# Issuing the early gate/up weight loads from GpSimd's DMA queue in place of SyncE's

## Chip, cores and metric

The kernel runs on one core of one Trainium2 chip. The metric is device time in microseconds (us); lower is better. Every kernel was run several times. A ratio is the mean time of one kernel's fast runs over the mean time of the other's fast runs of the same rounds, so it is not quite the ratio of the medians that are quoted beside it. The record marks each run as fast or as fallen into a slower state of the chip.

## The reference

```python
def reference(A_x, A_wqkv, A_wo, B_x, B_W_gate, B_W_up, B_W_down):
    # x: 1 x 2048 x 1024, bf16;  W_gate, W_up: 1024 x 3584;  W_down: 3584 x 1024
    x = A_x
    h  = x + attn(_layernorm(x), A_wqkv, A_wo)      # linear attention, 32 heads of 32
    h2 = h + ffn(_layernorm(h), B_W_gate, B_W_up, B_W_down)
    return h2
    # attn: num/den of phi(q)·(phi(k)^T v), then @ wo
    # ffn:  (relu(x @ W_gate) * (x @ W_up)) @ W_down
```

(Shortened: `attn` and `ffn` stand for the code of the two blocks.)

## The kernel before

The matrix products are done in blocks by Strassen's scheme. Between about 150 and 291 us of the span one stage mixes two things. Token blocks of 128 go through attention: `nd` and `attn` matmuls, the residual, the second layernorm. Beside them run the last q projections (`L438`) and the first gate/up products (`L705`, "early quads"), which fill TensorE. The weights of these early quads come in eight loads of 512 KB. This is the part that loads them:

```python
def hold(dst, src):
    nc.gpsimd.tensor_copy(out=dst, in_=src)            # 1x1 copy, L142

def load_group(g):
    for nm, v in (("wg", wg_v), ("wu", wu_v)):
        w_sb = wpools[g % 2].tile([P, KC, 2, GP * P], BF16, tag=nm, name=nm)
        for h in range(2):
            def load(after=None, w_sb=w_sb, v=v, h=h):
                if after is not None:
                    hold(w_sb[0:1, 0, h, 0:1], after)  # paces the load
                nc.sync.dma_start(out=w_sb[:, :, h, :],            # L486
                                  in_=v[:, :, h, g * GP * P:(g + 1) * GP * P])
            ...
# in the loop over attention steps:
        attn_step(step)
        if step:
            for _ in range(-(-len(early_loads) // (QSTEPS - step))):
                early_loads.pop(0)(held[step][0:1, 0:1])   # after = an element of this step's o_sb
```

So a load goes out only when a 1x1 copy has read this step's attention output `o_sb`. Eight loads are paced over seven steps; I call them the first to the eighth. The SyncE queue also carries everything that a token needs:

```python
nc.sync.dma_start_transpose(out=st["oT"], in_=st["o"][:])                  # L525, "oT transpose"
nc.sync.dma_start(out=x_sb[:], in_=xf[t * P:(t + 1) * P, :])               # L529
nc.sync.dma_start(out=h_dram[i][s][:, r // P, :], in_=h_sb[:])             # L546
# second layernorm: VectorE writes the mean (L551), then ScalarE:
st["hn"] = bwork.tile([P, D], BF16, tag="hn", bufs=HB, name="hn")          # HB = 2 buffers
nc.scalar.activation(out=st["hn"][:], in_=h_sb[:], func=ACT.Square, ...)   # L553
...
nc.sync.dma_start_transpose(out=hnT[s][i][:, :, r:r + P], in_=st["hn"][:]) # L560, "hn transpose"
```

Two users wait for an hn transpose. ScalarE can write an `hn` buffer again (`L553`) only when the transpose has read it, and there are two buffers. VectorE's sums `hs` (`L117`) and the early quads on TensorE read what it wrote.

## Time and profile before

| | before |
|---|---|
| time, median of 3 runs | 745.43 us (742.85 to 746.01) |
| span of the profiled run | 740.6 us |
| PE busy | 721.8 us, 97% |
| attention stage, 152.64 to 291.11 us | 138.47 us, PE idle 7.08 us in it |
| second hn transpose, issue to landing | 4.9 us |

From the page of before: the busy time of each engine, and the chain of waits by engine. In the first line, PE is TensorE's matmuls and PEld its weight loads.

```profile
...
PE 721.8 (97%) x3967; PEld 382.0 (52%) x4020; DVE 563.2 (76%) x991; ACT 322.0 (43%) x580; POOL 5.7 (1%) x44
...
PE 78%; DVE 8%; ACT 7%; DMA 5%; issue 2%; SPq 0%; DVEq 0%; POOL 0%; ACTq 0%
...
```

TensorE bounds the kernel. The next fence is one row of the table of stretches of before: the attention stage, from the issue of the first oT transpose to the first matmul of the next stage (`accA`). PEclk is the clock that the throttle granted TensorE, as a share of full speed.

```profile
...
core 0: us, PE busy (x) PEld busy (x) DVE busy (x) ACT busy (x) POOL busy (x), PEclk, DMA share, GB/s
152.64:291.11 138.47, 131.39 (x669) 62.04 (x681) 104.27 (x262) 95.16 (x241) 1.89 (x8) 1.00 0.75 175
...
```

138.47 less 131.39 gives 7.08 us of idle TensorE, at full clock. The next fence holds a line of the SyncE queue's own waits between 150 and 210 us: total, times, longest. This wait for GpSimd's pacing copies is what the change aims at.

```profile
...
SPq L486 <- POOL wu L142: 8.0, 3, 5.8
...
```

The last two fences are from the timeline of before: start, duration, engine and line. In brackets is how long the engine had waited, and for what. First, the second hn transpose and what hangs on it:

```profile
...
175.92 1.43 SPq L560 DMA_TRANSPOSE hn<-hn  x1
...
177.44 0.58 SPq L486 DMA_DIRECT2D wg<-in_B_W_gate_dram  x1
...
180.90 1.15 ACT L553 ACTIVATE hn<-x_res,sm 128x1024 bf16<-128x1024 bf16 x1 [0.74 <-DMA hn<-hn]
...
186.28 1.46 PE L438 MATMUL Aq<-xT,tq 128*128 128x512 bf16 x5 [1.10 <-ACT u L154]
...
```

The sixth load stands behind the hn transpose on the queue, issued 1.5 us later. ScalarE waits 0.74 us for the transpose (buffer reuse). ScalarE works in order, so its next copy of a PSUM tile (`u`, `L154`) is late, and TensorE waits 1.10 us for that. Second, the eighth load and the fifth hn transpose:

```profile
...
198.19 0.38 SPq L486 DMA_DIRECT2D wu<-in_B_W_up_dram  x1
...
200.97 1.68 SPq L560 DMA_TRANSPOSE hn<-hn  x1
...
204.93 0.43 DVE L117 TENSOR_TENSOR hs<-hn 128x512 f16<-128x512 bf16 x1 [0.26 <-DMA hn<-hn]
...
```

Here the load was issued 2.8 us ahead, and VectorE waits 0.26 us for the transpose.

### The profile page before, as it was taken

The numbers are of one execution on the slowest core, as the hardware profiler recorded it, in microseconds if no ns is written. First come the engines' busy times: TensorE is split into PE (matmuls) and PEld (weight loads), VectorE is DVE, ScalarE is ACT, GpSimd is POOL, SyncE is SP. The second block draws the span as 40 slices with busy tenths as digits, with TensorE's granted clock in tenths as the row PEclk, the third lists the DMA queues.
The fourth block names the chain that finished last, engine by engine and source line by source line (L and its number), as shares of the span: only waits on it lengthen the run. The fifth ranks groups of instructions, "written<-read, shape, count | busy, mean of one in ns | idle before, by whom it ended". The sixth has DMA issues, their size and how long they took to land.

```text
span 740.6 us, 10570 instructions
## 1 busy us (share of the span) xinstructions
PE 721.8 (97%) x3967; PEld 382.0 (52%) x4020; DVE 563.2 (76%) x991; ACT 322.0 (43%) x580; POOL 5.7 (1%) x44
## 2 busy tenths in 40 slices
PE   7999999999989999999999999999999999999997
PEld 3444555444444444444444444444444458888666
DVE  6997653675887767778778777877787479996797
ACT  4786553778686654444344434443435120000000
POOL 0000000000000000000000000000000000000000
PEclk9999999999999999999999999999999999999999
DMA  9765003079797526164638359475483399988822
GB/s 319 167 140 157 0 1 107 9 155 242 152 223 165 138 73 203 46 181 137 196 127 233 109 181 288 162 221 201 170 271 127 124 396 345 326 286 298 300 79 79
DMA packets 146579, 132.03 MB, mean 178 GB/s; under 512 B 50912, under 2 KB 128096, under 8 KB 146528
## 3 DMA queue, kind: packets, MB, share of 16 engines
q1 hardware_dynamic: 135392, 123.23, 55.3%
q10 hardware_dynamic: 11136, 8.13, 3.4%
q8 instruction: 31, 0.51, 0.3%
q14 instruction: 20, 0.16, 0.1%
HBM read 79.95 MB, written 39.85 MB: 162 GB/s over the span
## 4 chain that ended last, share of the span: by engine, by line
PE 78%; DVE 8%; ACT 7%; DMA 5%; issue 2%; SPq 0%; DVEq 0%; POOL 0%; ACTq 0%
PE accA L785 22%; PE accX L785 8%; PE accY L785 8%; PE accA L1117 8%; PE Aq L298 3%; PE accA L946 3%; PE accX L1117 3%; PE Aq L438 3%; DMA hn<-hn 2%; PE accY L1117 2%; PE attn L541 2%; PE Aq L705 2%; PE Eq L298 2%; PE accY L946 2%; PE accX L946 2%
## 5 line engine op out<-in xcount | busy, mean ns | idle before, releaser
L795 ACT ACTIVATE gu<-gu 128x512 bf16<-128x512 bf16 x72 | 45.4, 631 | 131.5 <-DVE gu L794 131.5
L790 ACT COPY snap<-accA 128x1024 f32<-128x1024 f32 x72 | 72.5, 1008 | 36.3 <-PE accA L785 36.2
L785 PEld LDWEIGHTS <-tg 128*128 128x128 f16 x384 | 37.6, 98 | 45.3
L785 PEld LDWEIGHTS <-tu 128*128 128x128 f16 x384 | 37.6, 98 | 45.3
L541 PE MATMUL attn<-wo_mem,oT 128*128 128x512 bf16 x249 | 57.9, 379 | 1.2 <-DVE o_sb L518 0.4
L794 DVE TENSOR_TENSOR gu<-accY,snap 128x1024 bf16<-128x1024 f32 x36 | 43.9, 1219 | 10.0 <-ACT snap L790 10.0
L785 PE MATMUL accA<-hn,tu 128*128 128x512 f16 (+1 forms) x192 | 49.3, 379 | 0.0
L785 PE MATMUL accA<-hn,tg 128*128 128x512 f16 (+1 forms) x192 | 49.3, 379 | 0.0
L794 DVE TENSOR_TENSOR gu<-accX,snap 128x1024 bf16<-128x1024 f32 x36 | 43.9, 1219 | 6.2 <-PE accX L785 3.7
L154 ACT COPY u<-Aq 128x512 f32<-128x512 f32 x56 | 32.4, 582 | 37.3 <-PE Aq L298 19.3
L1117 PEld LDWEIGHTS <-x 128*128 128x128 f16 (+1 forms) x448 | 43.8, 98 | 5.5
L785 PEld LDWEIGHTS <-wg 128*128 128x128 bf16 x288 | 28.2, 98 | 34.0
L785 PEld LDWEIGHTS <-wu 128*128 128x128 bf16 x288 | 28.2, 98 | 34.0
L541 PEld LDWEIGHTS <-oT 128*128 128x128 bf16 x256 | 24.6, 98 | 30.8 <-issue 2.9
L798 DVE TENSOR_TENSOR hq<-gu 128x512 bf16<-128x512 bf16 x48 | 20.3, 423 | 14.3 <-ACT gu L795 14.2
L298 PEld LDWEIGHTS <-xT 128*128 128x128 bf16 (+1 forms) x192 | 18.6, 98 | 23.7 <-issue 2.3
L1117 PEld LDWEIGHTS <-xs 128*128 128x128 f16 x280 | 27.4, 98 | 3.2
L543 DVE SCALAR_TENSOR_TENSOR x_res<-attn,x_res 128x512 bf16<-128x512 f32 x32 | 21.8, 687 | 7.2 <-PE attn L541 7.1
L946 PEld LDWEIGHTS <-x 128*128 128x128 bf16 (+1 forms) x168 | 16.4, 98 | 19.6
L518 DVE TENSOR_TENSOR o_sb<-nd,rd 128x384 bf16<-128x384 f32 (+1 forms) x48 | 22.8, 507 | 4.5 <-ACT rd L517 4.4
L1123 DVE TENSOR_TENSOR snap<-accA,u 128x1024 f32<-128x1024 f32 x16 | 19.5, 1220 | 8.3 <-PE accA L1117 8.0
L785 PE MATMUL accA<-hn,wu 128*128 128x512 bf16 x96 | 24.6, 379 | 0.0
(232 smaller groups left out, 1400.8 us busy)
## 6 DMA issues: line engine op xcount, KB each, us to landing
x<-x_dram SPq DMA_DIRECT2D x17, 896.0 KB, 8.2
x_dram<-hq SPq DMA_DIRECT2D x28, 512.0 KB, 3.1
wg<-in_B_W_gate_dram SPq DMA_DIRECT2D x14, 512.0 KB, 5.2
wu<-in_B_W_up_dram SPq DMA_DIRECT2D x14, 512.0 KB, 7.3
wraw<-in_B_W_down_dram SPq DMA_DIRECT2D x14, 512.0 KB, 4.8
x_dram<-hq SPq DMA_DIRECT2D x28, 256.0 KB, 2.6
t_dram<-wt SPq DMA_DIRECT2D x28, 256.0 KB, 2.2
xd<-x_dram SPq DMA_DIRECT2D x6, 896.0 KB, 7.1
```

The source lines that it names most:

```text
L154: nc.scalar.copy(out=snaps[nm, v], in_=A[v][:])
L298: nc.tensor.matmul(ps[:], lhsT=left[m - 1][:, kc, r + v * P:r + (v + 1) * P], rhs=right[m - 1][:, kc, :], start=(start and kc == 0), stop= ...
L438: nc.tensor.matmul(ps[:], lhsT=rq[m - 1][:, kc, (c + v) * P:(c + v + 1) * P], rhs=left[m - 1][:, kc, :], start=(start and kc == 0), stop=( ...
L518: nc.vector.tensor_tensor(out=ov[:, c0:c0 + n], in0=ndv[:, :, 0:P].rearrange("p k (h e) -> p k h e", h=HPC), in1=rd[:, 0:n, :].unsqueeze(3 ...
L541: nc.tensor.matmul(ps[:], lhsT=st["oT"][:, c, :], rhs=wo_sb[:, c, j * NW:(j + 1) * NW], start=(c == 0), stop=(c == KC - 1))
L543: nc.vector.scalar_tensor_tensor(out=h_sb[:, j * NW:(j + 1) * NW], in0=ps[:], scalar=1.0, in1=h_sb[:, j * NW:(j + 1) * NW], op0=ALU.mult, ...
L785: nc.tensor.matmul(ps[:, v, :], lhsT=w[v][n - 1][:, kc, :], rhs=left[n - 1][:, kc, :], start=(t is not None and kc == 0), stop=(kc == KH - ...
L790: nc.scalar.copy(out=st[nm][:], in_=halves(st["A"]))
L794: add(out=g[:], in0=halves(st[nm]), in1=st[base][:], op=ALU.add)
L795: nc.scalar.activation(out=g[:, 0, :], in_=g[:, 0, :], func=ACT.Relu)
L946: nc.tensor.matmul(ps[:, t * NW:(t + 1) * NW], lhsT=x_tile(n, s, kh)[:, f, (t0 + t) * P:(t0 + t + 1) * P], rhs=w_tile(n, kh)[:, f, :], sta ...
L1117: nc.tensor.matmul(pv[:, tt, :], lhsT=left(m)[:, f, tt * P:(tt + 1) * P], rhs=right(m)[:, f, :], start=(t is not None and f == 0 and tt % ...
```

## The change

The intent is to take the eight paced loads off the SyncE queue, where waiting for the pacing copy blocks the transposes behind. GpSimd makes the copy anyway, so it can issue the load right behind it.

```diff
                 def load(after=None, w_sb=w_sb, v=v, h=h):
                     if after is not None:
                         hold(w_sb[0:1, 0, h, 0:1], after)
-                    nc.sync.dma_start(out=w_sb[:, :, h, :], in_=v[:, :, h, g * GP * P:(g + 1) * GP * P])
+                    (nc.sync if after is None else nc.gpsimd).dma_start(out=w_sb[:, :, h, :], in_=v[:, :, h, g * GP * P:(g + 1) * GP * P])
```

The scheduler also reorders a little. On VectorE the first of the four `hs` sums (`L117`) of the fifth token moves ahead of the mean (`L551`) of the sixth, and the same happens once more two tokens later; some weight sums move later, and two neighbouring groups of matmuls swap on TensorE. ScalarE's order stays.

## The prediction

> **What bounds the kernel now.** TensorE. The page of before gives PE 721.8 us busy of a 740.6 us span (97%), clock 1.0, and the chain of waits is 78% PE. The change touches only the attention/early-quad stage, about 150 to 292 us. By the table of stretches PE is idle about 7 us of 142 there: 1.2 us in 170-190, 2.7 in 210-220, 1.2 in 260-280, the rest in crumbs. A perfect repair is worth 7 us (0.9%); 2% (15 us) is out of reach.
>
> **What it removes.** Eight loads of 512 KB leave the SyncE queue. In the queue's own waits they stood 8.4 us for the GpSimd copies (longest 5.8, ending at 198.2 us); their issue took 0.37 to 0.58 us each, about 3.7 us. Transposes queued near them took 1.75 to 3.24 us to issue where others take 1.23; about 7 us more. SyncE is relieved of 15-19 us between 153 and 200 us.
>
> **What of that is critical.** Little. Most waits of that queue are for data (37.3 us for o_sb). After the longest block (192-198 us) the next attention transpose needed an o_sb that VectorE finished at 199.6, and issued at 199.68. One hn transpose, ready at 198.3, issued at 200.97: 2.6 us earlier is possible. But VectorE is packed from 193 to 205 (9.4-9.5 busy of 10), so the next token's statistics come no sooner. The wait at 220.3 us (PE 2.0 us for the hs sums) ends on the transpose issued at 215.62, when no load is left in either kernel. The 1.1 us wait at 186.3 goes back to an hn transpose (175.92, 4.9 us to land) that shares the DMA engines with a load; the Trainium skill's "DMA: Bandwidth & Descriptors", section "Issuing engines are not separate DMA queues", says that the engines stay shared whoever issues. Expected gain: 0 to 2 us.
>
> **What it adds.** GpSimd, idle here but for eight copies of 0.18-0.3 us, now generates descriptors: 1024 rows of 512 B per load. Before has no such issue; call its duration T. GpSimd is in order, so each copy waits for the issues ahead, and the built code makes VectorE's write of an o_sb buffer wait for the copy that read it two steps before. From before's times (first copies 153.4, o_sb writes 169.5, 174.6, 186.9, 197.2) I estimate that T up to 7 us costs nothing (153.4+3T < 174.6); the weights are first needed at 193.7, so four loads fit up to T of 10. My guess for T is 1.5 to 5 us. The Trainium skill's "SBUF — State Buffer", the box on the "DVE blocks DMA" trap, says that VectorE's two-port modes starve such issues; before cannot show it. Scheduling also moves one hs sum ahead of a token's statistics on VectorE (0.5 us either way).
>
> **Predicted.** 744.5 us (745.43 before), 739.5 to 751.5 eight times in ten. Faster by over 2%: 0.01; within 2%: 0.94; slower: 0.05.
>
> **What would show it.** SyncE's waits for these copies gone, transposes near 1.23 us; eight DMA issues on GpSimd of 1.5-5 us; PE busy unchanged; idle in 150-292 us still 5-9 us; the wait of about 2 us for hs before the first Eq sums still there; stages after 292 us alike but shifted.
>
> **What would make it wrong.** T above 7 us: o_sb writes wait for GpSimd, PE for nd and attn, and tens of us may go. Descriptor writing that slows VectorE's two-input operations (their means would rise). Or an hn loop really SyncE-bound, when up to 5 us come back.

## The result, and the profile after

| | before | after |
|---|---|---|
| time, median of 4 runs of the same rounds | 744.65 us (742.85 to 746.01) | 755.0 us (754.65 to 755.37) |
| ratio, 95% interval | | 1.0141 [1.0116, 1.0165] |
| span of the profiled run | 740.6 us | 753.1 us |
| PE busy | 721.8 us | 729.8 us |
| attention stage | 138.47 us | 150.74 us |
| second hn transpose, issue to landing | 4.9 us | 7.2 us |

The change costs 10.4 us by the medians, outside the predicted range. From the page of after, the busy line and the new queue of GpSimd (packets, MB, share of the 16 engines):

```profile
...
PE 729.8 (97%) x3967; PEld 384.2 (51%) x4020; DVE 563.0 (75%) x991; ACT 322.0 (43%) x580; POOL 12.9 (2%) x52
...
q0 software_dynamic: 1152, 4.19, 2.3%
...
```

The two traces lack the same number of matmul records (3967 of 4020 are there), so their PE times can be compared: 8.0 us more for the same work. VectorE's busy time did not grow. In the view of the load's line after (durations min/median/max in ns), GpSimd's issuing is short and even:

```profile
...
L486 POOL DMA_DIRECT2D wg<-in_B_W_gate_dram x4: 882/883/1018, 153.9 to 176.0; - x4
L486 POOL DMA_DIRECT2D wu<-in_B_W_up_dram x4: 882/883/884, 158.1 to 203.8; - x4
...
```

SyncE's waits for the copies are gone. So the change did what it was meant to do, and the loss is elsewhere. These are rows of the table of stretches of after: the attention stage, then four of the stretches of 2 us around its first stall (columns as in before):

```profile
...
152.91:303.65 150.74, 138.36 (x669) 63.97 (x681) 104.14 (x262) 95.19 (x241) 9.08 (x16) 0.94 0.68 161
...
186.00:188.00 2.00, 0.26 (x2) 0.00 (x0) 1.04 (x2) 2.00 (x3) 0.00 (x0) 0.91 0.29 106
188.00:190.00 2.00, 0.92 (x2) 0.40 (x3) 1.24 (x4) 1.76 (x9) 0.00 (x0) 0.50 0.46 125
190.00:192.00 2.00, 2.00 (x6) 0.73 (x5) 1.39 (x3) 1.24 (x2) 1.06 (x2) 0.50 0.72 145
...
194.00:196.00 2.00, 2.00 (x10) 0.88 (x9) 1.13 (x4) 0.00 (x0) 0.00 (x0) 0.88 1.22 162
...
```

The stage took 12.27 us more, which is the whole difference of the spans within 0.3 us. PE idle in it is 150.74 - 138.36 = 12.38 us, so 5.3 us more. The same 669 matmuls took 138.36 - 131.39 = 7.0 us longer: the clock was halved three times. Before had 1.00 in all these rows. The timeline of after, the first stall:

```profile
...
175.99 0.88 POOL L486 DMA_DIRECT2D wg<-in_B_W_gate_dram  x1 [0.30 <-POOL wg L142]
176.21 1.46 SPq L560 DMA_TRANSPOSE hn<-hn  x1
...
183.48 1.15 ACT L553 ACTIVATE hn<-x_res,sm 128x1024 bf16<-128x1024 bf16 x1 [3.06 <-DMA hn<-hn]
...
188.86 0.58 PE L438 MATMUL Aq<-xT,tq 128*128 128x512 bf16 x1 [2.60 <-ACT u L154]
...
```

The sixth load is now issued at the same moment as the hn transpose, not behind it. The transpose lands after 7.2 us instead of 4.9. ScalarE waits 3.06 us, TensorE 2.60 us, and the clock halves. The second stall:

```profile
...
203.79 0.88 POOL L486 DMA_DIRECT2D wu<-in_B_W_up_dram  x1 [0.30 <-POOL wu L142]
...
204.10 1.27 SPq L560 DMA_TRANSPOSE hn<-hn  x1
...
210.28 0.42 DVE L117 TENSOR_TENSOR hs<-hn 128x512 f16<-128x512 bf16 x1 [2.75 <-DMA hn<-hn]
...
210.86 1.15 ACT L553 ACTIVATE hn<-x_res,sm 128x1024 bf16<-128x1024 bf16 x1 [2.65 <-DVE sm L551]
211.35 0.34 PE L511 MATMUL nd<-kvz,pq_mem 128*128 128x132 bf16 x3 [2.79 <-DVE o_sb L518]
...
```

The eighth load again meets an hn transpose, whose landing took 6.2 us (3.9 before). VectorE waits 2.75 us for it. In the new order the mean `sm` stands behind the first of those sums, so ScalarE waits too, and TensorE 2.79 us.

The third stall, at 226 to 230 us, is of another kind, for before has it too. Here are TensorE's two waits at this place, before and then after:

```profile
...
218.06 0.28 PE L511 MATMUL nd<-kvz,pq_mem 128*128 128x132 bf16 x2 [0.76 <-DVE o_sb L518]
220.34 0.59 PE L705 MATMUL Eq<-hs,tg 128*128 128x512 f16 x2 [2.00 <-DVE hs L117]
...
```

```profile
...
227.91 1.17 PE L511 MATMUL nd<-kvz,pq_mem 128*128 128x132 bf16 x8 [1.89 <-DVE o_sb L518]
230.44 1.01 PE L705 MATMUL Eq<-hs,tg 128*128 128x512 f16 x2 [1.36 <-DVE hs L117]
...
```

Together they grew only from 2.76 to 3.25 us. What is new is the halved clock. VectorE waits 2.92 us for the hn transpose here (0.84 before), but that transpose is hardly later: it landed after 5.4 us, 4.7 before, and 5.5 in two kernels below that lose nothing (six_pool, hb3_before). So a late landing does not explain this third part.

### The profile page after: what moved, and what is told of

Read it like the earlier page. It is cut to its first block, busy times and chain, and to the rows that moved or that the text cites. A ratio compares the mean times of both kernels' runs of the same rounds, so it can differ in the third digit from the quotient of the medians.

```text
span 753.1 us, 10572 instructions
## 1 busy us (share of the span) xinstructions
PE 729.8 (97%) x3967; PEld 384.2 (51%) x4020; DVE 563.0 (75%) x991; ACT 322.0 (43%) x580; POOL 12.9 (2%) x52
## 4 chain that ended last, share of the span: by engine, by line
PE 79%; DVE 8%; ACT 6%; DMA 5%; issue 2%; SPq 0%; DVEq 0%; ACTq 0%
PE accA L785 22%; PE accY L785 8%; PE accX L785 8%; PE accA L1117 8%; PE Aq L298 4%; PE attn L541 3%; PE accA L946 3%; PE accX L1117 3%; PE Aq L438 3%; PE accY L1117 2%; DMA hn<-hn 2%; PE Eq L298 2%; PE Aq L705 2%; PE accY L946 2%; PE accX L946 2%
## 5 line engine op out<-in xcount | busy, mean ns | idle before, releaser
L541 PE MATMUL attn<-wo_mem,oT 128*128 128x512 bf16 x249 | 61.6, 396 | 1.0 <-DVE o_sb L518 0.4
```

What stands on the lines that cost most here:

```text
L541: nc.tensor.matmul(ps[:], lhsT=st["oT"][:, c, :], rhs=wo_sb[:, c, j * NW:(j + 1) * NW], start=(c == 0), stop=(c == KC - 1))
```

## The experiments

Theory A: a load that GpSimd issues no longer stands behind the hn transpose on the SyncE queue. It runs beside it, the transpose lands late, ScalarE or VectorE waits, TensorE gets a gap, and its clock halves. Rival B: the new order on VectorE costs the time. Rival C: descriptor writing slows VectorE; this fell at once (563.2 us busy before, 563.0 after). Rival D: loads from GpSimd cost, whenever they run.

The experiments start from before or from after and differ from them by what their diffs show. "Exact order" means that TensorE, VectorE and ScalarE were compared and have the same instruction order as the kernel named. Where loads are picked out, this numbering was added to the loader:

```diff
-                def load(after=None, w_sb=w_sb, v=v, h=h):
+                def load(after=None, w_sb=w_sb, v=v, h=h, k=4 * g + 2 * (nm == "wu") + h):
```

| run | time, median | before, same rounds | ratio [95%] | second hn transpose lands after |
|---|---|---|---|---|
| sp_behind | 744.1 | 744.26 | 0.9991 [0.9958, 1.0024] | 4.7 us |
| pool_old_order | 749.71 | 744.26 | 1.0061 [1.0025, 1.0097] | 7.3 us |
| one_pool5 | 752.0 | 744.26 | 1.0098 [1.0051, 1.0145] | 11.1 us |
| six_pool | 744.09 | 742.62 | 1.0011 [0.9993, 1.0029] | 4.8 us |
| two_pool | 757.68 | 742.62 | 1.0184 [1.0156, 1.0211] | 9.3 us |
| pool_landed | 747.72 | 742.62 | 1.0060 [1.0034, 1.0086] | 4.8 us |
| early_pool | 748.53 | 742.62 | 1.0068 [1.0052, 1.0085] | 4.2 us |
| sp_ahead | 747.63 | 743.94 | 1.0042 [1.0026, 1.0058] | 6.1 us |
| one_act5 | 745.82 | 743.94 | 1.0026 [1.001, 1.0041] | 6.7 us |
| sp_later | 743.75 | 744.35 | 0.9993 [0.9971, 1.0014] | 4.4 us |
| hb3_before | 743.2 | 744.4 | 0.9984 [0.9969, 0.9999] | 4.6 us |
| hb3_one5 | 747.92 | 744.4 | 1.0055 [1.0023, 1.0086] | 12.2 us |
| hb3_old | 748.39 | 744.4 | 1.0051 [1.0035, 1.0066] | 7.1 us |
| hb3 | 752.87 | 744.4 | 1.0116 [1.0086, 1.0145] | 11.7 us |

The landing is of the one profiled run of each. All outputs are right.

### Queue and order apart: sp_behind and pool_old_order

sp_behind has the new order and no load on GpSimd: the eighth load is written after the fifth hn transpose.

```diff
+            hn_ins.append(nc.sync.dma_start_transpose(...))   # hn_T keeps its instructions
...
+        with tc.issue_after(hn_ins[4].ins): early_loads and early_loads.pop(0)(held[QSTEPS - 1][0:1, 0:1])
```

> No load on GpSimd; all eight on SyncE, the last moved behind one hn transpose, which gives TensorE, VectorE and ScalarE exactly the instruction order of the changed kernel. Theory A: 742 to 746 us, clock 1.0, no PE idle above 3 us. Theory B: 750 us or more, with the wait of VectorE for an hn transpose in front of the statistics near 207 us.

pool_old_order is after with one ordering edge (no wait) that gives before's exact order:

```diff
-                    left_sums(hnT[n // STS], ...)
+                    (sums_after if n == 4 else left_sums)(hnT[n // STS], ..., *([st_ins[order[6]].ins] if n == 4 else []))
```

> All eight loads stay on GpSimd, but one ordering edge gives TensorE, VectorE and ScalarE exactly the instruction order of before. Theory A (a load from GpSimd overlaps a transpose that the SyncE queue used to keep ahead of it; the transpose lands late, PE stalls, its clock halves): the first stall near 186 us and the halved clock after it stay; the second one, where the statistics stood behind a late hs sum, shrinks: 748 to 753 us. Theory B (the new VectorE order does the harm): 743 to 746 us, no stall at 186 us. Theory C (descriptor writing slows VectorE): about 755 us, VectorE means up.

Measured: 744.1 us and 749.71 us. The new order alone costs nothing measurable, which refutes B as the first cause. The queue alone costs about 5.4 us. Both together cost about twice that, so the new order makes late transposes dearer: in the old order the second stall turned into a wait of 1.63 us for an oT transpose, without a drop of the clock.

### The collision by itself: bench

A DMA-only program timed a transpose of the same shape beside a load of the same 512 KB, six times each: alone, beside a load from GpSimd, beside one from ScalarE, behind a load on its own queue (`spfirst`), and ahead of it (`splast`). Its output is wrong, which doesn't matter for the time.

> A wrong result on purpose: only DMA, six times each. A 128x1024 transpose from SyncE, alone, with a 512 KB weight load issued at about the same moment from GpSimd or from the ScalarE queue, behind such a load on SyncE, and ahead of one on SyncE. Theory A: alone 3 to 3.5 us to landing, beside the GpSimd load 6 us or more, ahead of a load on SyncE 3 to 5. If the load's packet size matters (4 KB on the software queue, 512 B on the hardware queues), beside the ScalarE-queue load 5 us or less; if only a second queue matters, the same as beside GpSimd's. Rivals B and C: beside the GpSimd load no slower than beside the others.

Its DMA view: queues (packets, MB, share), then issues (count, median us from issue to landing).

```profile
...
q0 software_dynamic: 864, 3.15, 6.7%
q10 hardware_dynamic: 6240, 3.15, 6.2%
...
t_alone<-src SPq DMA_TRANSPOSE x6, 3.0
t_pool<-src SPq DMA_TRANSPOSE x6, 5.9
t_act<-src SPq DMA_TRANSPOSE x6, 4.9
t_spfirst<-src SPq DMA_TRANSPOSE x6, 4.4
t_splast<-src SPq DMA_TRANSPOSE x6, 3.1
```

A transpose ahead of a load on the same queue is as fast as alone. Behind it, beside ScalarE's load and beside GpSimd's load it gets slower in that order. The Trainium skill's "DMA: Bandwidth & Descriptors", section "Queues, rings and completion order", says that each DMA engine goes round between the queues that have work and drains a whole packet of one before it switches. Its section "SWDGE vs HWDGE vs iDMA" puts a packet of GpSimd's kind preferably at 4096 bytes or less. The traces agree as far as they go: here GpSimd's queue had 3.15 MB in 864 packets (3.6 KB on average), ScalarE's the same bytes in 6240 (about 500 bytes). By the kept trace, GpSimd's data packets have 4096 bytes and took 252 ns each on average, ScalarE's have 512 bytes and took 29 ns. The larger packets delayed the transpose more. That packet size is the reason is argued, not shown by itself.

### Which loads: one_pool5, six_pool, two_pool

The three differ in which loads GpSimd issues: the sixth (`k == 5`), all but the sixth and eighth, or only these two.

```diff
-                    nc.sync.dma_start(out=w_sb[:, :, h, :], ...)
+                    (nc.gpsimd if after is not None and k in (5,) else nc.sync).dma_start(out=w_sb[:, :, h, :], ...)
#   six_pool: k in (0, 1, 2, 3, 4, 6)      two_pool: k in (5, 7)
```

one_pool5 and six_pool have the exact order of before, two_pool that of after.

> Only one load, the second half of the second gate tile (issued near 176 us), goes to GpSimd; the order on TensorE, VectorE and ScalarE is exactly before's. Theory A: the hn transpose issued near 176.2 us lands in 6.5 us or more instead of 4.9, ScalarE waits 2 to 3 us for it, PE idles 3 us or more before 189 us and its clock halves; 748 to 752 us, about half of the whole loss from one load. Theory B: as before, 743 to 746 us.

> Six of the eight loads are issued by GpSimd; only the two that stood behind an hn transpose on the SyncE queue (the sixth and the eighth) stay there. The order of PE, VectorE and ScalarE is exactly that of before. Theory A (the loss comes from the two loads that overtake an hn transpose): 743 to 746.5 us, ratio within 0.3% of 1, no PE stretch with a clock of 0.5 in the attention stage, slowest hn landing at most about 5.2 us. Rival D (every load that GpSimd issues costs its share of the 5.4 us that all eight cost in the old order): about 748 us, ratio 1.005.

> Only the sixth and the eighth load are issued by GpSimd, in exactly the order of the changed kernel on PE, VectorE and ScalarE. Theory A: nearly all of the loss is here, 751 to 756 us, ratio 1.010 to 1.016, two or three stretches with the clock at 0.5 in the attention stage, an hn landing of 7 us or more. Rival D: a quarter of the loss, 746 to 748 us.

The timeline of one_pool5:

```profile
...
176.08 1.01 POOL L486 DMA_DIRECT2D wg<-in_B_W_gate_dram  x1 [0.30 <-POOL wg L142]
176.27 1.44 SPq L560 DMA_TRANSPOSE hn<-hn  x1
...
187.48 1.15 ACT L553 ACTIVATE hn<-x_res,sm 128x1024 bf16<-128x1024 bf16 x1 [6.98 <-DMA hn<-hn]
...
189.24 1.01 PE L438 MATMUL Aq<-xT,wq_sb 128*128 128x512 f16 x2 [4.57 <-ACT u L154]
...
```

This one load on GpSimd lost 7.7 us by the medians, with runs from 748.44 to 755.68 us. ScalarE waited 6.98 us (2 to 3 had been expected) and TensorE 4.57 us. By the medians this one load cost more than all eight in the same order (pool_old_order, 5.4 us, landing 7.3 us); the intervals overlap, and nothing here explains the longer landing. In the timeline of six_pool, the sixth load is back behind the transpose:

```profile
...
176.15 1.88 SPq L560 DMA_TRANSPOSE hn<-hn  x1
...
178.13 0.53 SPq L486 DMA_DIRECT2D wg<-in_B_W_gate_dram  x1
...
```

Six of the eight loads on GpSimd cost nothing measurable (1.0011, the interval holds 1), and the other two alone cost all of it and more (1.0184; 757.68 us is above the range that A had been given). That refutes D in this form: it depends on which transpose a load meets. Taking these six loads off the SyncE queue gains nothing either, since six_pool is not faster than before. (It keeps the longest wait for a copy, 5.8 us for the eighth load; sp_behind takes that one out of the transposes' way and is not measurably faster.)

### Keeping GpSimd, moving the moment: pool_landed and early_pool

pool_landed lets the sixth and eighth load start only when the hn transpose they used to stand behind has landed (the pacing copy reads its output). early_pool issues all eight from GpSimd before the first attention step, without pacing. Both have the exact order of after.

```diff
 # pool_landed
-                early_loads.pop(0)(held[step][0:1, 0:1])
+                early_loads.pop(0)(landed[1] if step == 5 else held[step][0:1, 0:1])
+        step == QSTEPS and early_loads.pop(0)(landed[4])       # the eighth
 # early_pool: the paced calls removed; these loads issued by GpSimd, ahead of the loop
+    [f() for f in early_loads]
```

> All eight loads are issued by GpSimd, in the order of the changed kernel on PE, VectorE, ScalarE and SyncE, but the sixth and the eighth load are released by a copy that reads the landed destination of the hn transpose they used to stand behind, so they can't run beside it. Theory A: 743 to 747.5 us, the hn landings back at 5.2 us or less, clock at 0.95 or more in the attention stage. Rival D (loads from GpSimd cost whenever they run): 750 to 755 us. A result between (747.5 to 750) would say that the oT transposes or the next hn transposes, which the later loads now meet, cost something too.

> All eight loads are issued by GpSimd without any pacing copy, before the first attention step, where the DMA engines are less busy and no hn transpose is in flight; orders of PE, VectorE, ScalarE and SyncE as in the changed kernel. Theory A: 742.5 to 746 us, no clock of 0.5 in the attention stage. Rival D: 750 us or more. If the loads collide with the transposes of the projection stage instead, the loss shows as PE idle before 152 us of the span.

pool_landed, 747.72 us, fell at the edge of the two ranges. The landing of the second hn transpose was back at 4.8 us and the first stall was gone. But the seventh load (issued at 187.90 us) now met the fourth hn transpose, which landed after 8.0 us (3.2 before), and the first early quad waited 2.3 us for it. The eighth load, held back, met the sixth hn transpose. Its timeline:

```profile
...
208.13 0.88 POOL L486 DMA_DIRECT2D wu<-in_B_W_up_dram  x1 [0.30 <-POOL wu L142]
...
208.73 1.27 SPq L560 DMA_TRANSPOSE hn<-hn  x1
...
215.16 0.43 DVE L117 TENSOR_TENSOR hs<-hn 128x512 f16<-128x512 bf16 x1 [3.48 <-DMA hn<-hn]
...
216.11 0.33 PE L511 MATMUL nd<-kvz,pq_mem 128*128 128x132 bf16 x3 [2.33 <-DVE o_sb L518]
...
```

early_pool missed its expected range: 748.53 us. Its first four loads (120.6 to 123.3 us), where no transpose was near, cost nothing: PE was busy 19.87 us between 110 and 130 us in both kernels. The last four had to wait for their buffers until 151.9 us and met the first oT transposes, which landed after up to 9.7 us. From its timeline:

```profile
...
159.72 0.56 DVE L518 TENSOR_TENSOR o_sb<-nd,rd 128x384 bf16<-128x384 f32 x1 [3.20 <-DMA oT<-o_sb]
...
160.33 1.89 PE L541 MATMUL attn<-wo_mem,oT 128*128 128x512 bf16 x7 [3.27 <-DVE o_sb L518]
...
```

So the harm comes with any transpose that is soon needed, oT or hn, and both kernels only moved the collision.

### Dose: sp_ahead, one_act5, sp_later

sp_ahead swaps the sixth load and the second hn transpose on the SyncE queue, so that the load is just ahead. one_act5 is one_pool5 with ScalarE as issuer. Its trace shows a few neighbouring ScalarE instructions near 185 us in another order than before's, so the queue is not all that differs. sp_later swaps the other way: the load goes behind the oT transpose that follows. sp_ahead and sp_later have before's exact order.

```diff
 # sp_ahead
-            nc.sync.dma_start_transpose(out=hnT[s][i][:, :, r:r + P], in_=st["hn"][:])
+            with tc.issue_after(<sixth or eighth load, popped here>.ins): <the same transpose>
 # one_act5
+                    (nc.scalar if after is not None and k in (5,) else nc.sync).dma_start(...)
 # sp_later
+                with tc.issue_after(oT_ins[5].ins): <the sixth load>
```

> No load on GpSimd. One swap on the SyncE queue against before: the sixth load is issued just ahead of the second hn transpose instead of just behind it, everything else in the order of before. It tells whether being overtaken hurts whatever the queue, or whether it takes a second queue. If the order of issue is all that matters: the hn landing grows from 4.9 to 6 us or more and the time to 747 to 752 us. If it takes another queue (the DMA-only program had 4.4 us for a transpose behind a load on its own queue, 5.9 us beside one from GpSimd): hn landing at most 6 us, 743 to 746 us.

> Only the sixth load leaves the SyncE queue, as in the earlier one-load run from GpSimd (752.0 us), but ScalarE issues it: a second queue with 512-byte packets instead of GpSimd's of about 3.6 KB. If any second queue does the harm: hn landing 6 to 11 us, 747 to 753 us. If GpSimd's large packets do it: hn landing up to about 6 us, 743 to 747 us. The DMA-only program (4.9 us beside ScalarE's load, 5.9 us beside GpSimd's) speaks for something between. ScalarE's own issuing may add up to 1 us to its order, one swap of which is forced by the scheduler.

> All loads on SyncE as before, with one swap in the other direction: the sixth load is issued behind the oT transposes that follow the second hn transpose, so the hn transpose has nothing large behind it for 2.5 us longer. PE, VectorE and ScalarE orders exactly as before. If the landing of that hn transpose is the lever: it falls from 4.9 us to 3.1 to 4.3 us, ScalarE's wait of 0.74 us and PE's of 1.10 us shrink or go, and the time is 0 to 2 us less than before (ratio 0.997 to 1.000). If the landing does not change, the load behind it was not what made it 4.9 us, and the ratio stays within the interval around 1.

The timeline of sp_ahead (its transpose has line 559):

```profile
...
176.09 0.39 SPq L486 DMA_DIRECT2D wg<-in_B_W_gate_dram  x1
...
176.53 3.50 SPq L559 DMA_TRANSPOSE hn<-hn  x1
...
182.72 1.15 ACT L553 ACTIVATE hn<-x_res,sm 128x1024 bf16<-128x1024 bf16 x1 [2.43 <-DMA hn<-hn]
...
188.10 1.50 PE L438 MATMUL Aq<-xT,tq 128*128 128x512 bf16 x5 [2.60 <-ACT u L154]
...
```

No second queue is needed for harm: one swap on the SyncE queue cost 3.7 us by the medians. ScalarE's queue cost about 2 us, less than GpSimd's 7.7 with the same load at the same moment. Its landing was 6.7 us against 11.1, so it lay between the two cases that were expected: the time as for harmless, the landing as for harmful. sp_later changed the landing from 4.9 to 4.4 us and ScalarE's wait from 0.74 to 0.21 us, but the time not measurably. So the landing of this one transpose, from last place on the queue to GpSimd, orders as 4.4, 4.9, 6.1, 6.7, 11.1 us. The time follows only from about 6 us on; below that the wait fits into slack, and the clock stays whole at this place. The times of sp_ahead and one_act5 are not in the order of their landings; the two differ by 1.8 us, of the size of one halved clock window (below), and the profiled run of sp_ahead has one such window more.

### The link through ScalarE's buffer: hb3_one5, hb3_old, hb3, hb3_before

By then it was open whether the late landing is the cause or only a sign. A third `hn` buffer takes ScalarE's wait away and leaves the DMA traffic:

```diff
+    hn3 = mctx.enter_context(tc.tile_pool(name="hn3", reuse_waits="tile", bufs=1))
-            st["hn"] = bwork.tile([P, D], BF16, tag="hn", bufs=HB, name="hn")
+            st["hn"] = bwork.tile(...) if order.index(t) % 3 else hn3.tile([P, D], BF16, tag="hn3", name="hn")
```

It was added to one_pool5, pool_old_order, after and before. In the first two and in before the compute engines keep their exact order; in hb3 the scheduler moved some instructions after about 205 us.

> Before with a third hn buffer, loads on SyncE; control. ScalarE's wait for an hn transpose at about 181 us (0.74 us) goes; both theories: 742 to 745 us, ratio 0.997 to 1.001.

> The sixth load alone on GpSimd (752.0 us without the third buffer), with a third hn buffer, same orders on PE, VectorE and ScalarE. Link through ScalarE's buffer wait: the hn transpose still lands late (7 us or more), ScalarE doesn't wait for it, PE gap of 4.6 us gone, no halved clock near 190 us, 743 to 747 us. Rival (late landing is only a sign): 750 to 755 us as before.

> All eight loads on GpSimd in the old order of VectorE (749.7 us without the third buffer), with a third hn buffer. Link through ScalarE: 744 to 747.5 us; what is left over 744 is the later stall at 209 to 226 us, which goes through the oT transpose and VectorE's hs sums. Rival: 749 to 751 us.

> The change itself (755.0 us) with a third hn buffer; the scheduler moves some instructions after about 205 us. Link through ScalarE for the first stall: it goes (3.5 to 5 us back). The second and third stalls, which go through VectorE's wait for hn in its hs sums, stay unless the new order moves them: 747 to 751 us. Rival: 753 us or more. Below 745 us would mean that all three stalls went through the buffer.

Timeline of hb3_one5:

```profile
...
176.73 1.42 SPq L560 DMA_TRANSPOSE hn<-hn  x1
...
183.52 5.31 SPq L560 DMA_TRANSPOSE hn<-hn  x1
...
197.35 1.86 PE L705 MATMUL Aq<-hn,wg 128*128 128x512 bf16 x4 [3.56 <-DMA hn<-hn]
...
```

The transpose landed after 12.2 us, and ScalarE no longer waited for it. PE was busy 19.74 of the 20 us from 170 to 190 us, where one_pool5 had 15.43, so that link is shown. (In hb3_before, TensorE's wait of 1.10 us at 186 us fell to 0.26 likewise.) But the median came back only from 752.0 to 747.92 us (ratios 1.0098 and 1.0055 in different rounds, their intervals overlapping), short of the expected 743 to 747. The next hn transposes stood behind on the queue, one taking 5.31 us to issue, and then the first early quad waited 3.56 us for its data, at 197 us. hb3_old and hb3 also missed their ranges, by 0.9 and 1.9 us, and show the same wait of a quad (1.17 and 2.83 us). The buffer moves the wait from reuse to data and makes it shorter; the transposes are late all the same. As a version to keep, hb3_before is at best 0.2% faster than before, and its upper limit is 0.9999.

### The clock

No run took the clock by itself; its share is read from the traces. Summing 2 us × (1 - PEclk) over the stretches of 2 us at the three stalls of after gives 3.42, 1.70 and 3.42 us of lost clock. At half speed that is 6.84, 3.40 and 6.84 us of time: two, one and two units of 3.4 us. The Trainium skill's "TensorE: Matmul & The Clock Gate", Part 1, says that the clock halves after an idle window of about 3.4 us, and that these windows run freely and do not start with the kernel. The unit agrees. The kept traces also list each stretch of full and of half clock; in after they last 180.91, 6.83, 17.07, 3.41, 13.65 and 6.83 us, then 518.83. In this and all other kernels here (bench left out) every stretch but the last is a whole multiple of 3.413 us, within 2 ns. So in these runs the clock changed only at fixed moments, 3.413 us apart.

Cut at these moments, the traces show what decided: the idle time of TensorE within one window, not the length of one wait. (Some matmul records are missing, so idle times are approximate.)

| kernel, window | longest wait that reaches into it | TensorE idle in the window | clock after it |
|---|---|---|---|
| after, 184.24 to 187.65 us | 2.60 us | 2.04 us | half |
| after, 208.13 to 211.54 us | 2.79 us | 2.79 us | half |
| after, 225.20 to 228.61 us | 1.89 us | 2.02 us | half |
| before, 215.83 to 219.25 us | 2.00 us | 1.67 us | full |
| early_pool, 155.40 to 158.81 us | 3.27 us | 1.76 us | full |
| early_pool, 158.81 to 162.23 us | 3.27 us | 1.56 us | full |

early_pool's wait of 3.27 us fell across two windows and left the clock at 1.00, while 1.89 us sufficed in the third stall of after. In the 16 profiled runs of all kernels but bench, 22 of the 23 halvings followed a window with at least 2.02 us idle (the other had 1.62), and where the full clock was kept, no window had more than 1.95. So when TensorE was idle for some 2 of the 3.4 us, the next window ran at half clock, and where the windows fell decided whether a given wait did that. Part of the halved time PE was idle anyway, so the matmuls lost 7.0 us of the 8.5. The four runs of after had a mean clock of 0.987 to 0.989, so the profiled one is no exception.

The same unit shows in the spread of before itself. In the five timed sets of experiments, its runs with a mean granted clock of 1.0 took 742.60 us on average (16 runs), those with 0.998 took 744.30 us (28 runs): 1.7 us, one window at half speed. And two of sp_ahead's six runs kept 1.0 and took 745.02 and 745.80 us; against 742.60 that leaves an estimated 2 to 3 us for its idle time alone.

## Why the prediction was wrong

- Right: TensorE is the bound; the SyncE waits for the copies went; VectorE's rate did not suffer; the new order alone costs nothing; the stages after are alike but shifted (the stage's 12.27 us are the whole difference); the weight loads were not late. The gain of at most 2 us from freeing SyncE was close: six_pool and sp_behind show none.
- Failed, and the cause: "What of that is critical". The prediction itself named the hn transpose at 175.92 us and took its landing of 4.9 us as given, because "the engines stay shared whoever issues". Shared they are: in bench a transpose took 4.9 or 5.9 us beside a load from another queue, not 3.0. But the queue had kept the load behind the transpose, and sharing from the first moment is worse: 7.2 us after, 11.1 in one_pool5, against 4.9. The wait of 1.1 us became 2.60 us. The prediction counted what the queue delays and not what it protects.
- Failed: "PE busy unchanged". It rose by 8.0 us, because the clock halved after three windows in which TensorE was idle for 2.0 us or more. This term was missing altogether, and it is the larger part: 7.0 us of the stage's 12.27, against 5.3 us of idle. The idle was given as 5 to 9 us and was 12.38. The first two stalls go back to the late transposes; the third, 3.4 of the 8.5 us of lost clock, does not go back to a late landing, as far as the record shows.
- Failed: "transposes near 1.23 us". After, one oT transpose took 4.58 us to issue (at 177.76 us) and one 3.63 (at 205.46), both while a load was in flight. The copies' wait had not been what made them long.
- Failed: the hs sums moved on VectorE, "0.5 us either way". With late transposes it is about 5 us: 755.0 us after, 749.71 in pool_old_order, though 744.1 in sp_behind.
- Mis-sized: T, guessed 1.5 to 5 us, was 0.88 to 1.02 us. That side of the risk was not the one that mattered.

Still open: why the landing beside a GpSimd load ranged from 7.1 to 12.2 us in kernels with nearly the same order; whether packet size alone makes GpSimd's queue worse than ScalarE's; why the third stall, which before has too, crosses into a halved clock in after (in hb3_before and sp_later the clock halved there as well, for one window, without a measurable loss); and how much of the loss of after would remain at a constant clock.

## What to carry to other kernels

Here the DMA queue was also an order of priority. Before moving a bulk load to another queue, look for the short, urgent transfer it now stands behind, and expect that one to land late. Read what waits for that transfer, through buffers too, and whether the added wait leaves TensorE idle for some 2 us within one window of 3.4 us: then each window at half clock costs another 1.7 us. A wait just under that may do so in some runs and not in others. If only some of the moved transfers meet an urgent one, moving each subset shows it in two runs.

## What the Trainium skill lacked or had wrong

- "DMA: Bandwidth & Descriptors", section "Issuing engines are not separate DMA queues": it says that starting DMAs on several engines saves only sequencer time. It does not say that it can cost: the queue's order is lost. A transpose ahead of a 512 KB load on the same queue landed after 3.1 us (3.0 alone), beside one from GpSimd after 5.9 us; in the kernel 4.9 us became 7.1 to 12.2.
- The same page, section "Queues, rings and completion order": the round by packets is described without its effect on latency by kind of queue. Here a second queue with packets of about 500 bytes gave 4.9 us and one with 3.6 KB gave 5.9 us.
- "SBUF — State Buffer", the box on the "DVE blocks DMA" trap: not seen in this kernel. With VectorE busy 75% of the span, eight GpSimd issues took 0.88 to 1.02 us each, the same as in bench, where VectorE is busy 8% of the span. Whether VectorE ran in the two-port modes meanwhile, the traces don't say.
- "TensorE: Matmul & The Clock Gate", Part 1: the unit of 3.4 us agrees (6.84, 3.40 and 6.84 us at half speed), but the window need not be idle throughout: 2.02 us idle of 3.41 was enough in after, and 1.67 in before was not.
